# A third unit's local attention as matmuls, with other loads, another add of x and another mask

## The chip, the cores and the metric

The kernel runs on one core of a Trainium2 chip. The metric is the device time of one execution in microseconds; the median of three runs of the kernel before is 886.51 us (883.26 to 886.59).

## What is computed

The input is q, k, v of 4 batches, 8 heads, 576 positions, 64 dimensions. The attention is a sum of two parts, and two MLPs follow. Cut to what matters:

```python
def sm_attn(qq, kk, vv):                     # softmax attention
    ...
q_d, k_d, v_d = means over 4 neighbouring positions
out_up  = np.repeat(sm_attn(q_d, k_d, v_d), 4, axis=2)     # global: 144 positions
mask = np.abs(pos[:, None] - pos[None, :]) < 4             # local: 7 keys per query
out_local = softmax(np.where(mask, scale * q @ k.T, -1e9)) @ v
x = (out_up + out_local) as 2304 tokens x 512
h = np.maximum(np.maximum(x @ w1, x @ w2), x @ w3)         # 512 -> 768
y = h @ w_out                                              # 768 -> 512
g = y @ w_in;  out = np.maximum(0.01 * g, g) @ w_out2      # 512 -> 2048 -> 512
```

## The kernel before

The 2304 tokens are worked in 8 units of 288, two to a batch (unit u is a half of batch u // 2). Each unit passes through 22 steps: 18 steps of the first layer (6 blocks of 128 columns times three weight matrices, 12 matmuls of 128x288 each, since every product is made of three terms of a high and a low part), and 4 steps of the second layer, 18 matmuls each. Steps are counted through, g = 22 u + s. After unit 7 the second MLP runs in chunks of 512 tokens.

In L1_mm (L738) TensorE multiplies xh and xl, the high and low part of x, by the weights into ps_h; L1_post takes the largest of three products (ACT copies the first, VectorE's hm takes the maximum, L755) and splits it into hh (ACT) and hl (GpSimd, L759). L2 (L768) makes ps_o, which ACT copies out to memory (x2d).

The local attention, a window of seven keys, is made in two ways.

- Units 0 and 1 (u < PEU): on TensorE, a pair of heads at a time. pl_C puts a band mask and the scores into ps_ls, VectorE takes maxima and sums, ACT the exponential, GpSimd normalises, pl_O transposes (ps_lt), pl_P multiplies by v (ps_lo), pl_Q adds the global part on VectorE into x32, pl_R and pl_S split it into xh (ACT) and xl (GpSimd).
- Units 2 to 7: in the local stream, 12 items, two to a unit. GpSimd makes qkprod (L291, three to an item), VectorE (L301) and ACT (L304) sum it to scores ls, VectorE applies the mask to 21 of 63 columns (L310), a short softmax follows, VectorE makes pvprod (L335) and sums it to O (L342), three each. qkprod and pvprod share three buffers. emit_T then transposes O on TensorE (ps_x, L697, nine of them in three groups over two PSUM slots), VectorE adds the global part (L718) into the tile x32, ACT makes xh (L725), GpSimd xl (L726).

The global attention (names with ds) is made per batch and pair of heads: GpSimd or VectorE pools q and k (dsqk) and v (dsv), TensorE makes ps_sc, ps_aT and ps_up.

The order comes from three places. Up to the first layer of unit 0 a string, ORDER, lists the stages head by head, and all engines keep the order of the code. From then on only the queue of loads (SP) keeps it; the other engines are ordered by a scheduler before the run, and at run time each works through its own list in order. What is given to the scheduler at which step is set by tables: DONE and U1 spread the pieces of the local stream over the steps (the pools of the first way are released at step U1 = 15 and the stream's pools take their place), TURN says when emit_T of a unit comes, DS0 and DSOFF when the stages of the global attention come. The lines on which most rests:

```python
sl = s[:, 0:RC, :] if half == 0 else s[:, RU - RC : RU, :]
V.tensor_tensor(out=sl, in0=sl, in1=masks[half], op=ALU.min)
at(TURN[u], lambda u=u: emit_T(u))
```

## Time and profile before

| | |
|---|---|
| median of three runs | 886.51 us (883.26 to 886.59) |
| profiled execution, time | 885.25 us |
| its span | 883.4 us |
| mean granted clock of TensorE | 0.951 |
| TensorE busy | 825.4 us, 93% |
| VectorE busy | 490.2 us, 55% |
| ACT busy | 409.4 us, 46% |
| GpSimd busy | 292.0 us, 33% |

The time of an execution is a little more than the span of its instructions, here by 1.85 us. The shares are means over stages that differ much: in the page's 40 slices of 22 us TensorE is at 90% or more in most, and lower at the start and between the eighth and the thirteenth slice. What bounds a stage is read from that stage.

The names of the profile: PE is TensorE (its matmuls), PEld its weight loads, DVE VectorE, ACT ScalarE, POOL GpSimd, SP the engine that issues loads. A tile stands as out<-in by the program's names, L with a number is a line of the kernel.

### The profile page before, as it was taken

To read this page: it belongs to the slowest core of one execution; us is meant where nothing else is said; L and a number is where in the kernel's file an instruction comes from. 1 tells how busy PE (TensorE), PEld (TensorE's weight loads), DVE (VectorE), ACT (ScalarE), POOL (GpSimd) and SP (SyncE) were. 2 spreads that over 40 slices of the span, in tenths; PEclk is the share of its full clock that TensorE was granted. 3 is DMA by queue.
4 is the path that set the end of the run, shared out by engine and by line. 5 is a ranking of instruction groups with operands and counts; after the bars stand their busy time and mean duration, and the time that the engine had idled before them with its cause. 6 is when DMAs were issued, how large, how long until landed. Compare 5 with 4: busy or idle time off the path is not lost.

```text
span 883.4 us, 13548 instructions
## 1 busy us (share of the span) xinstructions
PE 825.4 (93%) x4886; PEld 726.5 (82%) x4890; DVE 490.2 (55%) x880; ACT 409.4 (46%) x1537; POOL 292.0 (33%) x263
## 2 busy tenths in 40 slices
...
GB/s 254 263 286 28 171 112 73 177 115 86 161 84 83 121 103 1 76 45 7 195 48 216 383 1 1 81 15 1 1 23 73 1 1 30 42 1 1 27 22 24
DMA packets 30486, 75.78 MB, mean 86 GB/s; under 512 B 3412, under 2 KB 8916, under 8 KB 30420
## 3 DMA queue, kind: packets, MB, share of 16 engines
...
q14 instruction: 29, 0.23, 0.1%
...
## 4 chain that ended last, share of the span: by engine, by line
PE 84%; DVE 6%; DMA 4%; ACT 3%; issue 1%; SPq 1%; ACTq 0%; DVEq 0%
PE ps_h L738 26%; PE acc L841 21%; PE ps_g L817 21%; PE ps_o L768 8%; DMA raw<-x2d 2%; PE ps_up L651 2%; DVE ls L310 2%; PE ps_sc L577 2%; ACT qkprod L304 2%; PE ps_lo L504 1%; PE ps_aT L629 1%; DMA skr<-in_kTp_dram 1%; PE ps_ls L429 1%; DVE x L718 1%; DVE pvprod L335 1%
## 5 line engine op out<-in xcount | busy, mean ns | idle before, releaser
L738 PE MATMUL ps_h<-xh,wA 128*128 128x288 f32 x1152 | 201.5, 306 | 17.9 <-ACT xh L725 10.9
L738 PEld LDWEIGHTS ps_h<-xh,wA 128*128 128x128 f32 x1152 | 172.4, 195 | 22.6 <-ACT xh L725 11.4
L841 PE MATMUL acc<-w2o,gh 128*128 128x512 f32 x576 | 178.1, 391 | 1.0 <-ACT gh L828 0.9
L817 PE MATMUL ps_g<-x2h,w2i 128*128 128x512 f32 (+1 forms) x640 | 158.9, 370 | 0.0
L825 DVE TENSOR_TENSOR g<-g,ps_g 128x512 f32<-128x512 f32 (+1 forms) x80 | 50.7, 634 | 185.1 <-ACT g L824 185.0
L817 PEld LDWEIGHTS ps_g<-x2h,w2i 128*128 128x128 f32 x640 | 114.6, 188 | 22.9
L824 ACT ACTIVATE g<-ps_g 128x512 f32<-128x512 f32 (+1 forms) x80 | 44.3, 553 | 186.2 <-PE ps_g L817 186.2
L841 PEld LDWEIGHTS acc<-w2o,gh 128*128 128x128 f32 x576 | 106.8, 188 | 23.8 <-ACT gh L828 1.9
L291 POOL TENSOR_TENSOR qkprod<-lq,lk 128x1344 f32<-128x1344 f32 x36 | 110.4, 3073 | 12.4 <-DVE O L342 4.4
L738 PE MATMUL ps_h<-xl,wA 128*128 128x288 f32 x576 | 113.6, 303 | 0.0
L841 PE MATMUL acc<-w2o,gl 128*128 128x512 f32 x288 | 112.2, 391 | 0.1
L738 PEld LDWEIGHTS ps_h<-xl,wA 128*128 128x128 f32 x576 | 90.9, 194 | 0.8 <-issue 0.8
L304 ACT ACTIVATE qkprod<-qkprod 128x64 f32<-128x64 f32 x364 | 87.6, 248 | 2.9 <-POOL qkprod L291 2.8
L755 DVE TENSOR_TENSOR hm<-hm,ps_h 128x288 f32<-128x288 f32 x96 | 43.0, 448 | 70.7 <-PE ps_h L738 65.3
L817 PE MATMUL ps_g<-x2l,w2i 128*128 128x512 f32 (+1 forms) x320 | 79.6, 370 | 0.0
L768 PE MATMUL ps_o<-hh,wO 128*128 128x288 f32 x384 | 75.3, 296 | 0.0
L829 DVE TENSOR_TENSOR gl<-g,gh 128x512 fp32r<-128x512 f32 (+1 forms) x80 | 51.0, 638 | 39.6 <-ACT gh L828 35.1
L759 POOL TENSOR_TENSOR hl<-hm,hh 128x288 fp32r<-128x288 f32 x48 | 40.5, 844 | 95.0 <-ACT hh L758 94.2
L304 ACT ACTIVATION_READ_ACCUMULATOR qkprod<-qkprod 128x1 f32 x364 | 70.6, 194 | 0.0
L828 ACT ACTIVATE gh<-g 128x512 fp32r<-128x512 f32 (+1 forms) x80 | 47.0, 588 | 42.7 <-DVE g L825 42.3
L817 PEld LDWEIGHTS ps_g<-x2l,w2i 128*128 128x128 f32 x320 | 56.8, 188 | 10.9
L841 PEld LDWEIGHTS acc<-w2o,gl 128*128 128x128 f32 x288 | 54.1, 188 | 12.6 <-DVE gl L829 0.9
...
## 6 DMA issues: line engine op xcount, KB each, us to landing
...
lv<-in_vL_dram SPq DMA_DIRECT2D x12, 480.0 KB, 4.6
lk<-in_k_dram SPq DMA_DIRECT2D x11, 480.0 KB, 4.5
...
```

The source lines that it names most:

```text
L291: P.tensor_tensor(out=pr, in0=in0, in1=in1, op=ALU.mult)
L304: A.activation(out=pr[:, r, j], in_=pr[:, r, j], func=AF.Copy, accum_out=sc[:, r, j : j + 1])
L738: T.matmul(out=ps, lhsT=wA[m, e][wi][:, kk * 128 : kk * 128 + 128], rhs=xx[:, kk] if u < PEU else xx[:, :, kk, :], start=n == 0, stop=n == ...
L755: V.tensor_tensor(out=t, in0=t, in1=ps, op=ALU.max)
L759: P.tensor_tensor(out=hl[:, m], in0=t, in1=hh[:, m].bitcast(F32), op=ALU.subtract)
L768: T.matmul(out=ps, lhsT=wO[m][wi][:, os_], rhs=xx[:, m], start=n == 0, stop=n == 3 * M1 - 1)
L817: T.matmul(out=ps, lhsT=w2i[m][wi][:, kk * 128 : kk * 128 + 128], rhs=xx[:, kk, :n], start=j == 0, stop=j == 3 * KC - 1,)
L824: A.activation(out=g, in_=ps, func=AF.Copy, scale=0.01)
L825: V.tensor_tensor(out=g, in0=g, in1=ps, op=ALU.max)
L828: A.activation(out=gh, in_=g, func=AF.Copy)
L829: V.tensor_tensor(out=gl, in0=g, in1=gh.bitcast(F32), op=ALU.subtract)
L841: T.matmul(out=accs[c, t], lhsT=a[:, ts], rhs=w, start=m == 0 and j == 0, stop=m == M2 - 1 and j == 2)
```

## The change

- PEU goes from 2 to 3: unit 2, the first half of batch 1, makes its local attention on TensorE, and batch 1's global attention is put into the same steps, 12 to 35 (table B1), that is beside units 0 and 1. The stages of unit 1 come one step later than before. dsqk of batch 1 is summed by VectorE (before, by GpSimd).
- The local stream has 10 items (6 to 15) and starts at step SUP = 37. Unit 3, the first of them, is laid out over contiguous positions ("whole"): its additions of the global part are 15 small ones.
- q and k of a pair of heads come in one load (tile sqk), v of both halves of a batch in one (sv, 344 KB in place of 168 KB ahead of the weights from the fourth on). The host lays out q, k, v of the local stream by lanes (qL, kL, vL), a load each.
- emit_T adds the global part to ps_x in place in PSUM; ACT makes xh from PSUM, and VectorE xl (before, GpSimd, from the tile x32). The slot of ps_x is in use until xl is done.
- The mask is 0 or a large negative number, added by GpSimd (before, the smaller of score and a large number, on VectorE).
- ON_A, the share of the score sums that ACT makes, holds for all items; in before the first four items had a smaller one. The string ORDER is arranged anew; in it the scores C of unit 1's first head come after twelve ps_h, where before they came ahead.

```diff
--- before.py
+++ after.py
-PEU = 2
+PEU = 3
-U1 = 15
+SUP = 37
...
-DONE = {2: 39, 3: 59, 4: 79, 5: 100, 6: 121, 7: 142}
-TURN = {2: 41, 3: 62, 4: 82, 5: 103, 6: 124, 7: 145}
-DS0 = {1: (15, 18, 21, 24), 2: (27, 38, 49, 60), 3: (68, 79, 90, 101)}
...
-ON_A_EARLY = (0, 7, 14)
+DONE = {3: 61, 4: 81, 5: 102, 6: 122, 7: 143}
+TURN = {3: 63, 4: 83, 5: 104, 6: 125, 7: 146}
+B1 = (12, 16, 20, 24)
+B1OFF = dict(A=0, v=1, C=1, B=2, L=4, O=6, M=7, P=9, N=10, Q=11)
+DS0 = {2: (39, 46, 53, 60), 3: (68, 79, 90, 101)}
 ON_A = (0, 21, 14)
...
-        P.memset(mk, 3.0e38)
+        P.memset(mk, 0.0)
...
-        V.tensor_tensor(out=sl, in0=sl, in1=masks[half], op=ALU.min)
+        P.tensor_tensor(out=sl, in0=sl, in1=masks[half], op=ALU.add)
...
+    def pl_load(what, b, h):
+        if what == "a":
+            t = sup.tile([128, 2 * S + 6], F32, tag="sqk", bufs=4, name="sqk")
+            nc.sync.dma_start(out=t, in_=qk[b, h])
+            dst[b, h, "q"], dst[b, h, "k"] = halves(t)
+            pl[b, h, "q"], pl[b, h, "k"] = t[:, :S], t[:, S:]
+        elif what == "s":
+            t = sup.tile([KP, 2, NBLK, 128], F32, tag="sv", bufs=4, name="sv")
+            n = PEU - 2 * b if b else 2
+            nc.sync.dma_start(
+                out=t[:, :n].rearrange("p u n d -> p (u n d)"), in_=vW[b, h][:, : n * NBLK * 128]
+            )
+            pl[b, h, "v"] = t
...
-            if b == 0:
+            if b < 2:
                 V.tensor_reduce(out=t[:, j], in_=raw, axis=AX.X, op=ALU.add)
...
-        groups = ((0, 4), (4, 8), (8, 9)) if half == 0 else ((0, 3), (3, 7), (7, 9))
+        whole = u == PEU
+        groups = ((0, 3), (3, 7), (7, 9)) if half and not whole else ((0, 4), (4, 8), (8, 9))
...
+                if whole:
+                    at_ = [(RU * c + r) // FAC for c in range(4)]
+                    for c0, nc_ in ((0, 4),) if len({at_[c + 1] - at_[c] for c in range(3)}) == 1 else ((0, 2), (2, 2)):
...
+                        V.tensor_tensor(out=sl, in0=sl, in1=in1, op=ALU.add)
...
-                sl = slice(r - g0, e - g0)
-                V.tensor_tensor(
-                    out=x32[:, sl].rearrange("p r (a c) -> p r a c", c=2),
-                    in0=pt[:, sl].rearrange("p r (a c) -> p r a c", c=2), in1=in1, op=ALU.add,
-                )
+                sl = pt[:, r - g0 : e - g0].rearrange("p r (a c) -> p r a c", c=2)
+                V.tensor_tensor(out=sl, in0=sl, in1=in1, op=ALU.add)
                 r = e
-            x32f = x32.rearrange("p r n -> p (r n)")
+            ptf = pt.rearrange("p r n -> p (r n)")
             xhf = xh[:, g0:g1].rearrange("p r a g -> p (r a g)")
-            A.activation(out=xhf, in_=x32f, func=AF.Copy)
-            P.tensor_tensor(
-                out=xl[:, g0:g1].rearrange("p r a g -> p (r a g)"), in0=x32f, in1=xhf.bitcast(F32), op=ALU.subtract
+            A.activation(out=xhf, in_=ptf, func=AF.Copy)
+            V.tensor_tensor(
+                out=xl[:, g0:g1].rearrange("p r a g -> p (r a g)"), in0=ptf, in1=xhf.bitcast(F32), op=ALU.subtract
             )
...
-        for what in "q0 k0 q1 k1 p0 q2 k2 00 p1 q3 k3 01 w0 p2 02 w1 p3 03".split():
+        for what in "a0 a1 p0 a2 s0 p1 a3 s1 w0 p2 w1 s2 p3 w2 s3".split():
...
         for h in range(4):
-            at(3 * h, lambda h=h: [f(1, h) for f in (pl_C, pl_D, pl_E, pl_H, pl_I)])
-            at(3 * h + 4, lambda h=h: [f(1, h) for f in (pl_O, pl_o)])
-            at(3 * h + 5, lambda h=h: [f(1, h) for f in (pl_P, pl_Q, pl_R, pl_S)])
+            at(3 * h + 1, lambda h=h: [f(1, h) for f in (pl_C, pl_D, pl_E, pl_H, pl_I)])
+            at(3 * h + 2, lambda h=h: pl_load("a", 1, h))
+            at(3 * h + 5, lambda h=h: [f(1, h) for f in (pl_O, pl_o)])
+            at(3 * h + 6, lambda h=h: [f(1, h) for f in (pl_P, pl_Q, pl_R, pl_S)])
+            at(3 * h + 7, lambda h=h: pl_load("s", 1, h))
+        for h in range(4):
+            for w, fs in {
+                "A": lambda h: ds_pool_qk(1, h),
+                "v": lambda h: ds_load(1, h, "v"),
+                "C": lambda h: [f(2, h) for f in (pl_C, pl_D, pl_E, pl_H, pl_I)],
+                "B": lambda h: [f(1, h) for f in (ds_B, ds_F, ds_G, ds_J, ds_norm)],
+                "L": lambda h: ds_pool_v(1, h),
+                "O": lambda h: [f(2, h) for f in (pl_O, pl_o)],
+                "M": lambda h: [f(1, h) for f in (ds_M, ds_m)],
+                "P": lambda h: pl_P(2, h),
+                "N": lambda h: [f(1, h) for f in (ds_N, ds_v)],
+                "Q": lambda h: [f(2, h) for f in (pl_Q, pl_R, pl_S)],
+            }.items():
+                at(B1[h] + B1OFF[w], lambda h=h, fs=fs: fs(h))
```

Three places show what this does to the order. The first is TensorE where the first unit of the local stream begins. In before that is unit 2; the end of unit 1's second layer (ps_o) and the first ps_h of unit 2:

```order
L768 MATMUL ps_o<-hl,wO_1351 128x288 x4
L577 MATMUL ps_sc<-dsqk 72x144 x2
L651 MATMUL ps_up<-aT,dsv_1735 128x144 x4
L629 MATMUL ps_aT<-ident,dse 72x72 x8
L651 MATMUL ps_up<-aT,dsv_1865 128x144 x4
L629 MATMUL ps_aT<-ident,dse 72x72 x8
L651 MATMUL ps_up<-aT,dsv_1974 128x144 x4
L577 MATMUL ps_sc<-dsqk 72x144 x4
L697 MATMUL ps_x<-ident,O 128x128 x9
L738 MATMUL ps_h<-xh,wA_0_439 128x288 x4
L738 MATMUL ps_h<-xh,wA_1_454 128x288 x4
L738 MATMUL ps_h<-xh,wA_2_605 128x288 x4
```

And now, where it is unit 3, between unit 2's ps_o and unit 3's ps_h:

```order
L741 MATMUL ps_o<-hl,wO_1391 128x288 x4
L616 MATMUL ps_up<-aT,dsv_2451 128x144 x4
L594 MATMUL ps_aT<-ident,dse 72x72 x8
L542 MATMUL ps_sc<-dsqk 72x144 x4
L663 MATMUL ps_x<-ident,O 128x128 x9
L616 MATMUL ps_up<-aT,dsv_2647 128x144 x4
L711 MATMUL ps_h<-xh,wA_0_398 128x288 x4
L711 MATMUL ps_h<-xh,wA_1_658 128x288 x4
```

The nine ps_x and the wait for them moved from unit 2 to unit 3, and most of the global attention that stood ahead of them is gone from there: between unit 1's last ps_o and unit 2's first ps_h the new order has nothing.

The second place is VectorE around the additions of the global part for unit 3 (u1 and u2 have none of these now). Before, line L718, with the mask behind them:

```order
L335 TENSOR_TENSOR pvprod<-lp,lv 128x1344
L613 RECIPROCAL dssum<-ps_sc 72x2
L342 TENSOR_REDUCE O<-pvprod 128x3x64
L718 TENSOR_TENSOR x_2859<-ps_x,up 128x128
L718 TENSOR_TENSOR x_2859<-ps_x,up 128x256
L310 TENSOR_TENSOR ls<-ls,mask_80 128x21
L314 TENSOR_REDUCE lp<-ls 128x9
L315 TENSOR_TENSOR lp<-ls,lp 128x63
L718 TENSOR_TENSOR x_2867<-ps_x,up 128x256 x2
```

Now, line L682, in PSUM, with the pvprod of item 9 ahead of them and no mask:

```order
L282 TENSOR_REDUCE lp<-lp 128x9
L283 TENSOR_SCALAR lp<-lp 128x9
L284 RECIPROCAL lsm<-lp 128x9
L285 TENSOR_TENSOR lp<-lp,lsm 128x63
L295 TENSOR_TENSOR pvprod<-lp,lv 128x1344
L682 TENSOR_TENSOR ps_x<-ps_x,up 128x128 x2
L302 TENSOR_REDUCE O<-pvprod 128x3x64
L682 TENSOR_TENSOR ps_x<-ps_x,up 128x32x2 x2
L295 TENSOR_TENSOR pvprod<-lp,lv 128x1344
L682 TENSOR_TENSOR ps_x<-ps_x,up 128x32x2 x2
```

The additions stand in the queue behind ten pvprods, three each of items 6, 7 and 8 and one of item 9, and between further ones.

The third is GpSimd at the start of the local stream: before, the first products (qkprod), with no mask among them:

```order
L566 TENSOR_TENSOR dsqk<-dsraw 128x144 x2
L759 TENSOR_TENSOR hl<-hm,hh 128x288
L291 TENSOR_TENSOR qkprod<-lq,lk 128x1344 x3
L565 TENSOR_TENSOR dsraw<-dsraw 128x144x2 x2
L291 TENSOR_TENSOR qkprod<-lq,lk 128x1344
L549 TENSOR_TENSOR dsrawv<-dsrawv 72x4x128
L565 TENSOR_TENSOR dsraw<-dsraw 128x144x2
```

Now, with the first mask, L270:

```order
L251 TENSOR_TENSOR qkprod<-lq,lk 128x1344 x3
L732 TENSOR_TENSOR hl<-hm,hh 128x288
L251 TENSOR_TENSOR qkprod<-lq,lk 128x1344
L530 TENSOR_TENSOR dsraw<-dsraw 128x144x2 x2
L514 TENSOR_TENSOR dsrawv<-dsrawv 72x4x128
L251 TENSOR_TENSOR qkprod<-lq,lk 128x1344
L531 TENSOR_TENSOR dsqk<-dsraw 128x144
L530 TENSOR_TENSOR dsraw<-dsraw 128x144x2 x2
L531 TENSOR_TENSOR dsqk<-dsraw 128x144
L270 TENSOR_TENSOR ls<-ls,mask_80 128x21
```

The mask of an item stands behind the next item's first two products and the pooling of batch 2.

## Rows read from the trace of the kernel before

**Rows 1.** Windows: us busy per engine (instructions), TensorE's granted clock, DMA share, GB/s
```profile
160.00:180.00 20.00, 12.08 (x52) 9.77 (x52) 15.73 (x30) 12.32 (x69) 18.01 (x11) 0.50 0.56 190
180.00:200.00 20.00, 8.33 (x36) 7.00 (x36) 19.04 (x21) 7.80 (x54) 15.13 (x16) 0.50 0.33 111
200.00:220.00 20.00, 20.00 (x125) 18.99 (x124) 17.33 (x31) 13.08 (x89) 17.29 (x13) 0.83 0.28 95
240.00:260.00 20.00, 16.13 (x108) 14.77 (x107) 16.42 (x24) 9.41 (x52) 14.91 (x14) 0.91 0.39 136
```

**Rows 2.** Timeline of TensorE, 150 to 200: start, duration, instruction, wait before it
```profile
154.90 1.15 PE L651 MATMUL ps_up<-aT,dsv 72*128 72x144 f32 x8
...
193.82 4.21 PE L738 MATMUL ps_h<-xh,wA 128*128 128x288 f32 x16 [10.91 <-ACT xh L725]
```

**Rows 3.** Chain that ended last, 300 to 480: start, duration, what
```profile
308.32 1.80 PE ps_h L738 x12
...
355.55 13.55 PE ps_h L738 x100
...
436.11 28.80 PE ps_h L738 x216
...
474.49 9.77 PE ps_g L817 x43
```

**Rows 4.** Timeline of TensorE, 55 to 72
```profile
55.67 0.41 PE L421 MATMUL ps_ls<-band,ident_b 96*96 96x306 bf16 x1 [6.45 <-DVE wy L190]
...
57.28 0.61 PE L738 MATMUL ps_h<-xh,wA 128*128 128x288 f32 x1
...
63.35 0.29 PE L421 MATMUL ps_ls<-band,ident_b 96*96 96x306 bf16 x1
...
64.27 0.40 PE L738 MATMUL ps_h<-xh,wA 128*128 128x288 f32 x1
...
66.99 0.66 PE L484 MATMUL ps_lt<-ident,ple 96*102 96x96 f32 x6
...
69.11 1.48 PE L504 MATMUL ps_lo<-plt,sv 102*128 102x96 f32 x12
70.37 0.38 PE L738 MATMUL ps_h<-xh,wA 128*128 128x288 f32 x1
```

**Rows 5.** The page's list of DMAs: count, size, us to landing
```profile
lk<-in_k_dram SPq DMA_DIRECT2D x11, 480.0 KB, 4.5
```

**Rows 6.** Groups by line and form, 100 to 480: count, busy us, mean ns, waits
```profile
L291 POOL TENSOR_TENSOR qkprod<-lq,lk 128x1344 f32<-128x1344 f32 x36 | 110.4, 3073 | 12.4 <-DVE O L342 4.4 <-DVE ls L301 3.6 <-ACT qkprod L304 3.4
...
L342 DVE TENSOR_REDUCE O<-pvprod 128x192 f32<-128x1344 f32 x36 | 55.3, 1544 | 0.2
...
L755 DVE TENSOR_TENSOR hm<-hm,ps_h 128x288 f32<-128x288 f32 x86 | 38.5, 448 | 68.0 <-PE ps_h L738 62.8 <-ACT wl L185 2.6 <-ACT hm L752 2.2
L759 POOL TENSOR_TENSOR hl<-hm,hh 128x288 fp32r<-128x288 f32 x43 | 36.5, 849 | 94.8 <-ACT hh L758 94.2 <-DVE hm L755 0.6
...
L310 DVE TENSOR_TENSOR ls<-ls,mask 128x21 f32<-128x21 f32 x12 | 23.1, 1924 | 0.9 <-ACT qkprod L304 0.9
...
L301 DVE TENSOR_REDUCE ls<-qkprod 128x21 f32<-128x1344 f32 x12 | 18.5, 1546 | 6.5 <-POOL qkprod L291 6.5
...
L591 DVE TENSOR_REDUCE ps_sc<-ps_sc 72x2 f32<-72x288 f32 x24 | 10.8, 457 | 13.0 <-PE ps_sc L577 12.9
...
L301 DVE TENSOR_REDUCE ls<-qkprod 128x7 f32<-128x448 f32 x12 | 7.3, 608 | 0.1
...
L315 DVE TENSOR_TENSOR lp<-ls,lp 128x63 f32<-128x63 f32 x12 | 2.7, 222 | 0.2
...
L718 DVE TENSOR_TENSOR x<-ps_x,up 128x128 f32<-128x128 f32 x6 | 2.3, 386 | 4.5 <-PE ps_x L697 4.5
```

**Rows 7.** Tile pvprod: count, shortest, median and longest ns, first and last start
```profile
L335 DVE TENSOR_TENSOR pvprod<-lp,lv x36: 1533/1548/1561, 125.2 to 352.6; 128x1344 f32<-128x1344 f32 x36
```

**Rows 8.** Tile ls: the same for the mask
```profile
L310 DVE TENSOR_TENSOR ls<-ls,mask x12: 167/1238/6574, 110.5 to 339.7; 128x21 f32<-128x21 f32 x12
```

More of the change, by code (lines that the diff above doesn't have):

```diff
@@ L135, in local_global_attention_moe_kernel @@
     sup = tc.alloc_tile_pool(name="sup", bufs=1, side="left")
-    pools = {0: sup}
+    pools = {0: sup, 1: sup}
     bands = []
-    for u in range(PEU):
+    for u in range(2):
         bd = sup.tile([QB, NBLK, KB], BF16, name=f"band{u}")
@@ L298, in qk_reduce @@
         sc = loc[i, "s"][:, c * RC : c * RC + RC, :]
-        nv = RC * WIN - (ON_A_EARLY if i < 2 * I0 else ON_A)[c]
+        nv = RC * WIN - ON_A[c]
         if nv:
@@ L401, in pl_load @@
             dst[0, h, "vr"] = t
-        pl[h, what] = t
     def pl_pool_v(h):
@@ L421, in pl_C @@
             T.matmul(
-                out=t[:QB, :n], lhsT=ident_b, rhs=bands[u].rearrange("p n k -> p (n k)"), start=True, stop=False
+                out=t[:QB, :n], lhsT=ident_b, rhs=bands[u % 2].rearrange("p n k -> p (n k)"), start=True, stop=False
             )
         for j in range(NBLK):
-            s0 = u * NCOL + j * QB
+            s0 = u % 2 * NCOL + j * QB
             qs, ks = slice(s0, s0 + QB), slice(s0, s0 + KB)
@@ L540, in ds_load @@
             nc.sync.dma_start(out=t.rearrange("p c h f d -> p (c h f d)"), in_=vP[b, h])
+            dst[b, h, w] = t
         else:
-            t = pools[b].tile([128, SD, FAC], F32, tag="mid", bufs=4, name="dsraw")
-            nc.sync.dma_start(out=t.rearrange("p s f -> p (s f)"), in_=(qT if w == "q" else kT)[b, h])
-        dst[b, h, w] = t
+            t = pools[b].tile([128, 2 * S + 6], F32, tag="dsraw", bufs=2, name="dsraw")
+            nc.sync.dma_start(out=t, in_=qk[b, h])
+            dst[b, h, "q"], dst[b, h, "k"] = halves(t)
     def ds_pool_v(b, h):
@@ L659, in ds_v @@
         if h == 0:
-            up[b] = pools[b].tile([128, 4, SD], F32, tag="up", bufs=2 if b else 1, name="up")
+            up[b] = mmp.tile([128, 4, SD], F32, tag="up", bufs=2, name="up")
         for hh in range(2):
@@ L669, in ds_stages @@
         return [
-            lambda: [ds_load(b, h, w) for w in "qk"],
+            lambda: ds_load(b, h, "qk"),
             lambda: ds_pool_qk(b, h),
@@ L856, in L4 @@
                     steps = [[G * DM, e - a], [DM, G]] if u < PEU else [[DM, e - a], [R * DM, G]]
+                    if u == PEU:
+                        row, steps = u * NCOL + r, [[DM, e - a], [RU * DM, G]]
                     nc.sync.dma_start(
@@ L870, in local_global_attention_moe_kernel @@
             else:
-                pl_load(what[0], int(what[1]))
-        for t in W1[2:nl]:
+                pl_load(what[0], 0, int(what[1]))
+        for t in W1[3:nl]:
             load_w1(t)
-        for h in range(4):
-            pl_load("1", h)
         steps = {
@@ L919, in local_global_attention_moe_kernel @@
         pieces = list(local_stream())
-        g0 = U1
+        g0 = SUP
         for u in range(PEU, NU):
```

123 lines of the change are left out of this document (43 added, 80 removed), and 8 rows, old and new, of the table ORDER.

## The prediction

> **What bounds the kernel now.** I read the windows first. Between 160 and 260 us TensorE is not full: it is busy 12.08, 8.33, 20.00 and 16.13 of 20 us in the four windows shown, at a granted clock of 0.50, 0.50, 0.83 and 0.91 [rows 1]. VectorE is full there instead, 15.73 to 19.04 of 20. Later windows have TensorE full at clock 1.00, and the second MLP, from 474.49 on, is a row of matmuls without gaps, which the change does not touch. So the stage to look at is the one in which local attention passes from TensorE to the VectorE stream.
>
> TensorE instruction by instruction shows it [rows 2]. Unit 1's second layer ends at 154.90; what follows is the global attention of batch 1, unit 2's transposes (ps_x), and a wait of 10.91 us before its first ps_h at 193.82. It is put down to ACT's xh, which waits for VectorE's adds. Until then TensorE did in 38.9 us what needs about 9. The chain gives lengths of undisturbed units [rows 3]: unit 7 takes 474.49 - 436.11 = 38.4, of which 28.80 is the first layer (1.6 a step, 18 steps) and 9.6 the second; unit 4, which carries a batch's global attention and a transpose, takes 355.55 - 308.32 = 47.2. A batch's global attention therefore costs at most 8.8, and the stretch from unit 4's start to unit 7's end 166.2.
>
> The forecast is worked along TensorE: when unit 1 ends, when unit 2 ends, when unit 3's x is there, and what follows.
>
> **Until unit 2 starts.** The local attention of unit 2 is new work on TensorE. One head beside L1 costs: C (ps_ls) 64.27 - 63.35 = 0.92, twice; O (ps_lt) at most 0.66; P 70.37 - 69.11 = 1.26 [rows 4]. That is 3.8 a head, 15.0 for four. Batch 1's global attention, which stood behind 154.90, moves ahead of unit 1's end: 8.8. In the prologue the first ps_h stood behind C, which started at 55.67 after a wait of 6.45; now twelve ps_h stand ahead of it. That can give back at most 57.28 - 55.67 = 1.6 [rows 4]. Against it, 688 KB more of v are loaded ahead of the weights from the fourth on; I take a gain of 1.0, with 1.6 and -3 as ends. Unit 2 starts at 154.9 + 15.0 + 8.8 - 1.0 = 177.7. The one-load q and k and the host's lanes save issues on SP, which is waited for nowhere in this stretch: nothing.
>
> **Unit 2.** 38.4, plus about half of batch 2's global attention, 4.4 (its heads start at steps 39 to 60): it ends at 220.5. No ps_x stands before it, so the 38.9 us between [rows 2]'s two instructions go, but for the 8.8 counted above, and the half clock that followed goes too.
>
> **When unit 3's x is there.** The local stream starts at step 37, not 15, since its pools reuse those of the TensorE path. Its k load waits for the last xl of unit 2, step 35; four steps and a second layer, 4 x 1.6 + 9.6 = 16.0, lie between that and unit 2's start, and a k load lands 4.5 after its issue [rows 5]. First product on GpSimd: 177.7 - 16.0 + 4.5 = 166.2.
>
> From there it is a queue on GpSimd and then one on VectorE. Item 6's mask, now on GpSimd, stands behind five products of 3.07 and eight smaller steps; at hl's 0.85 for each [rows 6] it comes 22 us in, and with 2 us of softmax the first pvprod starts 24 us in. Unit 3's x adds stand on VectorE behind the tenth pvprod (items 6 to 8 and one of item 9). Between the first and the tenth the order has 9 pvprods of 1.55 [rows 7] and 9 O reduces of 1.54, 27.8; 3 score reduces of 1.55 and 3 of 0.61, 6.5; 18 softmax steps of 0.22, 4.0; 7 hm of 0.45, 3.1; 4 reduces of 0.46 and 16 tiny steps at 0.17, the shortest mask, 4.5: together 45.9 [rows 6 to 8]. VectorE was busy 68.5 of 80 us in [rows 1], and 95% in the window in which TensorE waited most; at 92% the 45.9 take 50. The adds come in 15 pieces with two pvprods, three O reduces, two score reduces and the three xl among them: 3.1 + 4.6 + 2.2, adds at 0.3 (0.39 for 128 columns, twelve are half as wide) 4.5, xl at most 1.8 by hm's 0.45 for 288 columns: 16.2, and 0.5 for xh. Unit 3 can start at 166.2 + 24 + 50 + 16.7 = 256.9, and TensorE waits 36 us, once, with only the tail of batch 2's attention to do.
>
> That xl goes from GpSimd to VectorE and now holds the PSUM slot until it is done is in these 16.2: the third transposes wait for the first xl. With two units in flight later it is covered by matmuls; uncovered it would cost one xl, 0.8 a unit.
>
> **After that.** The wait leaves the clock at half: after 193.82 the clock was 0.50 to 200 and 0.83 in the next window, 6.2 x 0.5 + 20 x 0.17 = 6.5 lost [rows 1]. Unit 3 takes 38.4 + 6.5 + 2.8 (a transpose and some global attention) = 47.7, units 4 to 7 the 166.2 of before. End of the first MLP: 470.8, 3.7 before the 474.49 of now. The small waits of unit 3 in before need no term, since 47.7 has none: most came behind long masks on VectorE, which go. From the profiled 885.25 this gives 881.5; it lies 1.3 under the median of the runs, and I say 881.
>
> **The mask.** VectorE's mask takes 1.92 us in the mean for 21 columns, 0.167 to 6.574 [rows 6, 8]: it is not work but waiting, and GpSimd was busy 15 to 18 of 20 us [rows 1]. On GpSimd I price it at 0.2, the shortest on VectorE; bounds are 0.17 and, if GpSimd waits in its place, 1.92. Its other price is order, the 22 us above.
>
> The Trainium skill (SBUF — State Buffer, section "Who interferes with whom") says that a VectorE tensor_tensor with both inputs in SBUF and a GpSimd instruction that reads SBUF exclude each other for a whole instruction, and that issue order decides who waits. The mask rows agree; pvprod, of the same kind, does not: all 36 lie between 1533 and 1561 ns [rows 7] beside a GpSimd as busy. By the rule pvprod and qkprod would keep taking turns, the mask's move would gain nothing, and the time would be the first rival's; by the rows it gains the 1.7 us an item.
>
> **Rivals.** *The stream keeps its pace.* In before a pvprod came every (352.6 - 125.2) / 35 = 6.5 us [rows 7]. Then the ten take 65 instead of 50, unit 3 starts at 272, and the end is at 485.8: 897. The break-even is 5.4 a pvprod. For it: products and pvprods still share three buffers, so each engine waits for the other, and GpSimd has the masks besides. Against it: 0.64 of the 6.5 was the mask, and part of the 36 were paced by TensorE's steps later on, where lateness cost nothing. The late start has no reserve: whatever the stream loses, TensorE loses one for one. Chance 0.25.
>
> *The stream runs at VectorE's rate.* First pvprod at 21, ten at 4.6, the adds in 12.5: unit 3 starts at 246 and the end is at 460, so 871. For it: TensorE asks for no hm while it waits, and there are no mask stalls. Against it: in-order queues on three engines, with an exp on ACT in each softmax. Chance 0.20.
>
> *Units 0 and 1 swell.* Two units with four heads took 97.6 in before, 76.8 + 15.0 and 5.8 of friction. With twice the heads, batch 1's attention and its pooling on VectorE, friction doubles: everything behind moves by 5.8, to 887. For it: each head is a chain through four engines, and a late one stops TensorE, which is in order. Against it: VectorE and GpSimd have no local stream there now. Chance 0.21. The forecast has 0.34.
>
> **How the numbers follow.** A measurement of this kernel tells 0.5%, 4.4 us, from no change. The forecast is 5 us under the median, its own range 874 to 888; of its 0.34 I count 0.24 as faster and 0.10 as no change. The second rival adds 0.20 faster. The third gives 0.19 no change and 0.02 slower, the first 0.23 slower and 0.02 no change. Sums: 0.44, 0.31 and 0.25. The range reaches from the second rival's 871, less the clock's 6.5 that a shorter wait would save in part, to just over the first's: 865 to 898.
>
> **What the profile after would show.** Right: no ps_x between unit 1 and unit 2, ps_h running on; one long idle on TensorE before unit 3's first ps_h, 30 to 40 us, released by ACT's xh, with the half clock around it and nowhere else before the second MLP; masks of 0.2 us on GpSimd; pvprods about 5 us apart until then. Wrong: a wait under 20 us with the first pvprods 4.6 apart (second rival), one of 45 or more with GpSimd and VectorE waiting for each other's products (first), or gaps of one or two us between the ps_h of steps 12 to 40 (third). An idle ahead of units 5 to 7 would say that the stream is too slow throughout, which I count out.

## The result: slower by 1.3%, and the profile after

The changed kernel took 898.05 us (median of 4, 895.51 to 899.23) beside 886.55 of the kernel before: ratio 1.0134, interval 1.0101 to 1.0167. The forecast of 881 was wrong in its sign; 898.05 lies 0.05 above the end of the stated range, beside the 897 of the first rival. The profiled execution took 899.23, 13.98 more than that of before.

The windows of the changed kernel, with the columns of [rows 1]:

```profile
180.00:200.00 20.00, 18.16 (x125) 17.32 (x124) 7.60 (x18) 11.98 (x81) 14.49 (x16) 0.91 0.18 63
200.00:220.00 20.00, 20.00 (x155) 19.82 (x155) 17.93 (x28) 12.62 (x88) 16.39 (x15) 1.00 0.33 111
220.00:240.00 20.00, 9.59 (x59) 7.56 (x57) 16.52 (x26) 12.48 (x87) 15.82 (x13) 0.72 0.52 174
240.00:260.00 20.00, 2.39 (x9) 1.75 (x9) 18.52 (x38) 14.09 (x105) 19.31 (x13) 0.50 0.21 76
...
300.00:320.00 20.00, 15.20 (x102) 14.16 (x102) 14.61 (x22) 13.11 (x86) 17.56 (x14) 0.86 0.41 141
320.00:340.00 20.00, 20.00 (x143) 19.30 (x143) 18.69 (x33) 13.01 (x88) 15.62 (x10) 0.97 0.33 106
```

The wait that stood at 160 to 200 in [rows 1] now stands at 225 to 263, as forecast. Below full again is 300 to 320, with TensorE busy 15.20 at clock 0.86; from 320 to 340 it is busy throughout at 0.97. In before both windows have 20.00 at 1.00. Instruction by instruction on TensorE, with the columns of [rows 2]:

```profile
179.56 0.80 PE L711 MATMUL ps_h<-xh,wA 128*128 128x288 f32 x4 [1.33 <-ACT ev L744]
...
186.71 0.81 PE L711 MATMUL ps_h<-xh,wA 128*128 128x288 f32 x4 [1.83 <-ACT ev L744]
...
224.38 0.69 PE L741 MATMUL ps_o<-hl,wO 128*128 128x288 f32 x4
...
245.03 1.94 PE L663 MATMUL ps_x<-ident,O 128*128 128x128 f32 x8 [5.08 <-DVE dssum L578]
258.91 0.45 PE L663 MATMUL ps_x<-ident,O 128*128 128x128 f32 x1 [11.94 <-DVE xl L699]
...
262.85 3.50 PE L711 MATMUL ps_h<-xh,wA 128*128 128x288 f32 x13
...
313.47 1.64 PE L711 MATMUL ps_h<-xh,wA 128*128 128x288 f32 x8 [3.46 <-ACT xh L698]
```

Unit 2 starts at 179.56 with no ps_x before it and a gap of 1.33; its last ps_o is issued at 224.38; unit 3's transposes come at 245.03, the last at 258.91, after 11.94 us for the slot that VectorE's xl holds; unit 3 starts at 262.85. Then unit 4 waits too, 3.46 for its xh, and 1.20 for ev. The starts of the units (first ps_h, from the timelines; the forecast's from its sum), us:

| | unit 2 | unit 3 | unit 4 | unit 5 | unit 6 |
|---|---|---|---|---|---|
| before | 193.8 | 250.7 | 308.3 | 355.5 | 396.5 |
| forecast | 177.7 | 256.9 | 304.6 | 351.8 | 392.9 |
| after | 179.6 | 262.9 | 313.5 | 365.0 | 410.7 |

From unit 6 on both kernels take the same. So 14.3 were gained by unit 2's start; the lead turned into 12.2 lost at unit 3's start, 5.2 lost at unit 4's, 9.5 at unit 5's and 14.1 at unit 6's.

### The profile page after: what moved, and what is told of

Same layout as the page of the kernel before. It is cut to its first block, busy times and chain, and to the rows that moved or that the text cites. A ratio compares the mean times of both kernels' runs of the same rounds, so it can differ in the third digit from the quotient of the medians.

```text
span 897.4 us, 13812 instructions
## 1 busy us (share of the span) xinstructions
PE 831.7 (93%) x5005; PEld 731.2 (81%) x5009; DVE 465.7 (52%) x912; ACT 414.7 (46%) x1556; POOL 258.6 (29%) x240
## 4 chain that ended last, share of the span: by engine, by line
PE 76%; DMA 8%; DVE 7%; ACT 3%; issue 2%; POOL 2%; SPq 1%; ACTq 0%; DVEq 0%; POOLq 0%
PE acc L814 21%; PE ps_g L790 21%; PE ps_h L711 20%; PE ps_o L741 6%; DMA lk<-in_kL_dram 2%; DMA x2d<-ev 2%; ACT qkprod L264 2%; PE ps_lo L468 1%; PE ps_up L616 1%; PE ps_sc L542 1%; POOL qkprod L251 1%; DMA raw<-x2d 1%; DMA wO<-in_w_out_dram 1%; PE warm_ps L166 1%; DVE pvprod L295 1%
## 5 line engine op out<-in xcount | busy, mean ns | idle before, releaser
L251 POOL TENSOR_TENSOR qkprod<-lq,lk 128x1344 f32<-128x1344 f32 x30 | 91.8, 3070 | 14.0 <-DMA lk<-in_kL_dram 4.8
L264 ACT ACTIVATE qkprod<-qkprod 128x64 f32<-128x64 f32 x350 | 84.1, 246 | 21.4 <-POOL qkprod L251 21.0
L741 PE MATMUL ps_o<-hh,wO 128*128 128x288 f32 x384 | 77.2, 297 | 0.0
L264 ACT ACTIVATION_READ_ACCUMULATOR qkprod<-qkprod 128x1 f32 x350 | 67.2, 192 | 0.0
```

The source lines that it names most:

```text
L251: P.tensor_tensor(out=pr, in0=in0, in1=in1, op=ALU.mult)
L264: A.activation(out=pr[:, r, j], in_=pr[:, r, j], func=AF.Copy, accum_out=sc[:, r, j : j + 1])
L741: T.matmul(out=ps, lhsT=wO[m][wi][:, os_], rhs=xx[:, m], start=n == 0, stop=n == 3 * M1 - 1)
```

## The experiments

Each kernel is the changed one with the edit that is named, unless it says "the kernel before". Ratios are to the kernel before, with the interval; the last columns are the starts of units from one profile. Every edit is scheduled anew, so the order of the engines moves with it. Counted in the traces, the additions of units 3, 4 and 5 begin behind 10, 19 and 27 pvprods in the changed kernel, 7, 19 and 26 in e1, 9, 19 and 26 in e3, 10, 18 and 25 in e4, 9, 18 and 26 in e5, 8, 16 and 24 in e15, 10, 17 and 25 in e16. No run holds the order fixed: a gain belongs to an edit together with the order that came with it.

| run | ratio | unit 3 | unit 4 | unit 5 | unit 6 |
|---|---|---|---|---|---|
| the change | 1.0134 (1.0101 to 1.0167) | 262.9 | 313.5 | 365.0 | 410.7 |
| e1 emit_T 61 | 1.0044 (1.0019 to 1.0069) | 244.7 | 307.8 | 355.9 | 400.8 |
| e2 emit_T 58 | 1.0118 (1.0058 to 1.0178) | 247.2 | 312.2 | 362.3 | 408.8 |
| e3 mask VectorE | 1.0047 (1.0007 to 1.0088) | 257.6 | 310.7 | 355.6 | 399.8 |
| e4 x SBUF, xl GpSimd | 0.9961 (0.9931 to 0.9990) | 257.0 | 307.6 | 353.4 | 396.9 |
| e5 e3 and e4 | 0.9974 (0.9937 to 1.0011) | 251.0 | 309.6 | 355.6 | 400.3 |
| e6 e5 and e1 | 1.0032 (0.9999 to 1.0064) | 240.9 | 314.3 | 361.5 | 404.3 |
| e7 x SBUF, xl VectorE | 1.0066 (1.0027 to 1.0105) | 255.9 | 307.0 | 358.9 | 401.7 |
| e8 two dsrawv | 1.0057 (1.0032 to 1.0083) | 260.4 | 311.8 | 359.4 | 404.9 |
| e9 four products | 1.0152 (1.0105 to 1.0199) | 257.0 | 310.1 | 368.6 | 414.8 |
| e10 e9 and e3 | 1.0041 (1.0006 to 1.0077) | 245.6 | 301.8 | 350.8 | 400.5 |
| e11 two pvprods | 0.9837 (0.9776 to 0.9898) | 244.3 | 294.2 | 340.1 | 385.7 |
| e12 two qkprods | 0.9968 (0.9939 to 0.9997) | 252.4 | 302.0 | 349.0 | 395.7 |
| e13 before, mask GpSimd | 0.9799 (0.9764 to 0.9834) | 236.7 | 283.9 | 333.9 | 376.7 |
| e14 before, x PSUM | 1.0078 (1.0050 to 1.0106) | 253.9 | 306.6 | 355.9 | 401.5 |
| e15 e4, 21 on ACT | 1.0005 (0.9983 to 1.0027) | 243.2 | 301.3 | 351.9 | 397.1 |
| e16 e4, 7 on ACT | 0.9929 (0.9902 to 0.9955) | 252.5 | 301.7 | 347.4 | 390.1 |
| e17 before, both edits | 0.9864 (0.9823 to 0.9905) | 241.2 | 291.4 | 339.4 | 386.1 |
| e18 e13, 7 on ACT | 0.9705 (0.9678 to 0.9731) | 236.9 | 283.5 | 329.6 | 373.2 |

**The order of unit 3's additions.** e1, and e2 with its stream pieces earlier too:

```diff
-TURN = {3: 63, 4: 83, ...
+TURN = {3: 61, 4: 83, ...
```

> The changed kernel with emit_T of unit 3 given to the scheduler two steps earlier (TURN 61 in place of 63). In the order unit 3's additions then stand on VectorE behind 7 pvprods in place of 10. Theory (order): the late start of unit 3 comes from the queue, in which work for unit 4 stands ahead of unit 3's additions. At the 5.3 us a pvprod that the changed kernel shows there, the additions come 3 x 5.3 = 16 us earlier, unit 3's first ps_h at about 247 in place of 262.9, and the time falls by 12 to 16, to 882 to 886. Rival (pace): the stream as a whole is too slow; unit 3 starts earlier, but units 4 and 5 wait for it by as much more, and the time stays at 894 to 898.

```diff
-DONE = {3: 61, ...
-TURN = {3: 63, ...
+DONE = {3: 57, ...
+TURN = {3: 58, ...
```

> The changed kernel with the pieces for unit 3 given to the scheduler by step 57 (DONE 57) and its emit_T at 58. The additions stand behind 6 pvprods, which is all of items 6 and 7 and nothing else, and the transposes ahead of unit 2's last four ps_o. Theory (order): another pvprod less, 5 us, so unit 3 starts 18 to 21 earlier than in the changed kernel, at 242 to 245, and the time is 877 to 882. Rival (pace): 892 to 898, with TensorE waiting before units 4 and 5. A third way: transposes that are not ready hold back ps_o on TensorE, and it is slower than with emit_T at 61.

Unit 3 started 18.1 earlier in e1, as the order theory has it, but unit 4 only 5.7 earlier. TensorE in e1, the same columns:

```profile
243.46 0.45 PE L663 MATMUL ps_x<-ident,O 128*128 128x128 f32 x1 [9.95 <-DVE lsm L284]
...
304.62 0.44 PE L663 MATMUL ps_x<-ident,O 128*128 128x128 f32 x1 [3.56 <-DVE xl L699]
...
307.77 1.57 PE L711 MATMUL ps_h<-xh,wA 128*128 128x288 f32 x5 [1.29 <-ACT xh L698]
```

The 11.94 before the last of unit 3's transposes became 9.95. Of the 18.1 us 12.4 were given back between unit 3's start and unit 4's: by the timelines 5.6 is a busy TensorE, with a head of the global attention that in the changed kernel stood ahead of unit 3, and 6.8 are waits, 4.7 of them ahead of a ps_up and 2.1 for xl and xh of unit 4 (5.6 in place of 3.5). So the order explains unit 3's start, and the pace only a part of what became of it; e1 kept 8 us of 18. In e2 the third way came true in part: it is slower than e1, and transposes wait for the slot for 18.7 us, in two pieces (waits of TensorE, 220 to 330):

```profile
PE ps_x L663 <- DVE xl L699: 18.7, 2, 13.3
```

**The two side edits undone.**

```diff
-        P.tensor_tensor(out=sl, in0=sl, in1=masks[half], op=ALU.add)
+        V.tensor_tensor(out=sl, in0=sl, in1=masks[half], op=ALU.min)
```

> The changed kernel with the mask as before: the smaller of score and large number, on VectorE. Theory (the mask's place in GpSimd's queue): the first pvprod came 30 us after the first product, of which 6 are the mask's wait behind products; they go, and unit 3 starts up to 6 earlier, 892 to 896. Rival (the shared access to SBUF): the mask on VectorE waits 1.9 us in the mean again, ten times, four of them before unit 3's additions, and it is slower by 4 to 8, 901 to 906.

```diff
+            x32 = mmp.tile([128, 512], F32, tag="x32t", bufs=2, ...)
-            V.tensor_tensor(out=sl, in0=sl, in1=in1, op=ALU.add)
+            V.tensor_tensor(out=so, in0=sl, in1=in1, op=ALU.add)     # so: in x32
-            V.tensor_tensor(out=xl..., in0=ptf, in1=xhf, op=ALU.subtract)
+            P.tensor_tensor(out=xl..., in0=x32, in1=xhf, op=ALU.subtract)
```

> The changed kernel with x as before: the sum goes to an SBUF tile, and GpSimd makes xl. Theory: the place of xl matters little, since three xl of 0.7 us stand in VectorE's queue; between 894 and 900. Rival: in the changed kernel the third group of unit 3's transposes waited 11.9 us for the first xl, which holds the PSUM slot; with an SBUF tile the slot is free after the additions, so unit 3 starts some us earlier and each later unit too: 888 to 893.

e3's mask waits on VectorE as before, up to 5.3 us (tile ls, columns of [rows 7]), and yet the kernel is 10 us faster than the changed one; its first pvprod starts at 190.8, 7 us earlier than in the changed kernel:

```profile
L270 DVE TENSOR_TENSOR ls<-ls,mask x10: 173/868/5319, 184.4 to 349.0; 128x21 f32<-128x21 f32 x10
```
```profile
L295 DVE TENSOR_TENSOR pvprod<-lp,lv x30: 1533/1551/1558, 190.8 to 361.1; 128x1344 f32<-128x1344 f32 x30
```

e4 gained more than its rival allowed, 15 us: the 11.94 before unit 3's last transpose became 1.73, and TensorE has no idle time left in units 4 and 5 (unit starts as windows, columns of [rows 1]):

```profile
307.57:353.44 45.87, 45.87 (x346) 44.42 (x346) 40.98 (x72) 35.44 (x227) 34.09 (x26) 1.00 0.23 72
353.44:396.91 43.47, 43.47 (x330) 42.74 (x329) 18.18 (x32) 11.30 (x33) 8.91 (x10) 1.00 0.19 64
```

Together they do not add, as e5 and e6 show:

> The changed kernel with both the mask on VectorE (e3) and x by an SBUF tile with xl on GpSimd (e4). Theory: two separate waits, the mask behind GpSimd's products and the PSUM slot held by ps_x; their effects (10 and 15 us) add in good part: 872 to 878. Rival: both only shorten the same wait, the late x of units 3 to 5, and together give hardly more than e4 alone: 880 to 884.

> e5 with emit_T of unit 3 two steps earlier as in e1: unit 3's additions stand behind 7 pvprods in place of 9. Theory (order): since units 4 and 5 now get their x in time, the 10 us that unit 3 starts earlier are kept at the end: 862 to 870. Rival (pace): as in e1 unit 4's start takes most of it back: within 3 us of e5.

e5 is no better than e4, as its rival says. A reason stands in its masks: with xl on GpSimd again, the ten masks on VectorE take 28.7 us (in e3 17.9), the longest 9.05 (columns of [rows 6]):

```profile
L270 DVE TENSOR_TENSOR ls<-ls,mask 128x21 f32<-128x21 f32 x10 | 28.7, 2867 | 0.8 <-ACT qkprod L264 0.8
```

In e6 unit 3 starts at 240.9, 22 earlier than in the changed kernel, and unit 4 at 314.3, later; it is 5 us slower than e5, which neither answer foretold, and it does not show the pace. Its masks take 37.6 us. One of them stands among unit 4's additions on VectorE; ACT's aT waits in order behind the softmax that follows it, and TensorE for aT:

```profile
301.21 6.90 DVE L270 TENSOR_TENSOR ls<-ls,mask 128x21 f32<-128x21 f32 x1
```
```profile
308.85 2.29 PE L616 MATMUL ps_up<-aT,dsv 72*128 72x144 f32 x8 [6.72 <-ACT aT L606]
```

The earlier emit_T with x in SBUF and the mask on GpSimd was not run. e7 parts what e4 joined (edit of e4, with xl left on V):

> The changed kernel with the sum written to an SBUF tile as before, but xl still on VectorE. It tells apart the two things that e4 undid. Theory (slot): what cost time is that ps_x keeps its PSUM slot until xl is done, so the next transposes and the global attention's ps_aT and ps_up wait; the gain of e4 stays with xl on VectorE: 882 to 887. Rival (engine): three xl of 0.7 us more per unit in VectorE's queue are what cost; 894 to 899.

At 892.59 (interval of the ratio 1.0027 to 1.0105) it lies between the two answers: by the ratios some 0.7% is the slot and 1.0% the engine of xl, each to about half a per cent.

**The queue of loads.**

```diff
-            t = pools[b].tile([QP, 2, 2, FAC, D], F32, tag="dsrawv", bufs=1, name="dsrawv")
+            t = pools[b].tile([QP, 2, 2, FAC, D], F32, tag="dsrawv", bufs=2, name="dsrawv")
```

> The changed kernel with two buffers in place of one for the tile dsrawv. In the changed kernel the queue of loads stood still for 83.7 us, up to 25.1 at a time, because a load of dsrawv waited until GpSimd had made dsv, and the next k loads of the stream stood behind it. Theory (load queue): with a second buffer those loads go out earlier, GpSimd no longer waits for lk, and units 4 and 5 get their x earlier: 890 to 894. Rival: loads are early enough, since GpSimd waited for lk for only 4.8 us in all: 896 to 899.

891.86, as the theory says of the time. GpSimd still waits 3.2 us for lk, in place of 4.8, and units 4 and 5 start 1.7 and 5.6 earlier. The wait of the loads (engine, line, releaser, us, times, longest), changed kernel and then e8:

```profile
SPq L504 <- POOL dsv L515: 83.7, 5, 25.1
```
```profile
SPq L504 <- POOL dsv L515: 30.8, 3, 14.3
```

It is not quite clean: in e8's order unit 3's additions stand behind 9 pvprods, not 10.

**What paces the stream.**

```diff
-        pr = pools["att"].tile([128, RC, WIN, D], F32, tag="prod", bufs=3, name="qkprod")
+        pr = pools["att"].tile([128, RC, WIN, D], F32, tag="prod", bufs=4, name="qkprod")
```

> The changed kernel with four buffers in place of three for the products (qkprod and pvprod share them). In all kernels so far unit 4 starts between 307 and 314 us, however early unit 3 starts (241 to 263), and an item of the stream takes 20.5 us in the changed kernel as in the one before. Theory (coupling): no engine is full, GpSimd and VectorE wait for each other's product buffers; a fourth one quickens the stream to 18 us an item or less, unit 4 starts before 306, and the time is 888 to 892. Rival (work): the stream is set by the sum of the instructions in VectorE's queue, and the buffer changes nothing: 896 to 899.

> e9 with the mask on VectorE as in e3. If the mask's place on GpSimd and the product buffers are two waits, their gains add to e3: 878 to 883. If both are the same waiting of VectorE for GpSimd's queue: as e3, 886 to 890.

(20.5 there is first product to last pvprod, divided by the items.) Coupling by the buffers falls: e9 is no faster than the changed kernel (901.53, above even the rival's range), and e10 is as e3. In e10 units 3 and 4 do start 12 and 9 us before those of e3, but unit 6 at 400.5 does not. The two probes take work away instead:

```diff
     def pv_mult(i, c):
+        if c == RU // RC - 1:
+            return
...
     def qk_mult(i, c):
+        if c == 1:
+            loc[i, "pr", 1] = loc[i, "pr0"]
+            return
```

> A probe: the changed kernel without the third pvprod and O sum of each item (ACT copies the first third of O in their place), 3.1 us an item less on VectorE, 31 in all. If VectorE's work sets the stream's pace, an item takes about 17 in place of 20.5 us, unit 4 starts 10 to 13 earlier (near 301), and the time falls by 12 to 16, to 882 to 886. If GpSimd sets it: under 4 us.

> A probe: the changed kernel without the second qkprod of each item (the score sums take the first product in its place), 3.1 us an item less on GpSimd, 31 in all, with every other engine's work as it is. If GpSimd's queue sets the stream's pace, an item takes about 17 us, unit 4 starts near 301 and the time is 882 to 886. If VectorE sets it: under 4 us, 895 to 899. If both e11 and e12 gain half of that, the two engines pace each other.

e11 gained 25 us, more than the 12 to 16 expected, e12 14 us, as expected if GpSimd sets the pace. So work taken from either engine shortens the time, from VectorE more; no one engine sets it alone. e11's pvprods, 20 in place of 30, end 26 us earlier than the changed kernel's:

```profile
L297 DVE TENSOR_TENSOR pvprod<-lp,lv x20: 1543/1554/1558, 198.7 to 346.2; 128x1344 f32<-128x1344 f32 x20
```

**The side edits by themselves,** in the kernel before (the edits of e3 and e4 the other way round):

> The kernel before with the mask as a sum on GpSimd and nothing else. Theory (queue): on GpSimd a mask stands behind products, and the softmax on VectorE behind it, in this kernel too; it costs 3 to 10 us: ratio to before 1.004 to 1.012. Rival (shared access): VectorE's 23 us of waiting in masks go, and units 2 to 4 get their x earlier: ratio 0.985 to 0.996.

> The kernel before with x added in PSUM and xl made by VectorE from it, and nothing else. Theory (slot and VectorE's queue): the slot of ps_x is held until xl is done and VectorE has 1.5 us more a unit; it costs here too, ratio 1.004 to 1.015. Rival: it costs only where x is late as in the changed kernel: ratio 0.998 to 1.002.

> The kernel before with both side edits, the mask on GpSimd and x added and split in PSUM, and units 0 and 1 alone on TensorE. If the edits add: 0.980 x 1.008 = 0.988 of before. If they hinder each other, as in the changed kernel, where the two together are slower than either alone: 0.995 or more. In the first case the changed kernel's loss against this one, 1.0134 / 0.988 = 1.026, is the third unit on TensorE with its late stream; in the second it is in good part the two edits.

The mask's move alone makes the kernel before 2.0% faster, against my theory. (In the two profiles 1.6 us of it stand already at unit 1's first ps_h, 110.94 against 112.58, ahead of the stream's first mask.) Its mask there (tile ls) and TensorE ahead of unit 2:

```profile
L310 POOL TENSOR_TENSOR ls<-ls,mask x12: 221/231/262, 116.0 to 322.7; 128x21 f32<-128x21 f32 x12
```
```profile
176.25 1.09 PE L697 MATMUL ps_x<-ident,O 128*128 128x128 f32 x4 [6.51 <-DVE ps_sc L612]
...
183.63 4.21 PE L738 MATMUL ps_h<-xh,wA 128*128 128x288 f32 x16 [4.30 <-ACT xh L725]
```

Of the 10.91 in [rows 2] 4.30 are left; the longest mask of before, 6.57 [rows 8], had stood in that wait. x in PSUM costs 0.8% there, and both together come to 0.9864, against 0.980 x 1.008 = 0.988: they add. Set side by side:

| | two units on TensorE | three units |
|---|---|---|
| mask VectorE, x in SBUF | 1 (before) | 0.9974 (e5) |
| mask GpSimd, x in SBUF | 0.9799 (e13) | 0.9961 (e4) |
| mask VectorE, x in PSUM | 1.0078 (e14) | 1.0047 (e3) |
| both | 0.9864 (e17) | 1.0134 (after) |

The third unit, with the loads and the order that belong to it, changes nothing while the mask is on VectorE (0.9974, and 1.0047 / 1.0078 = 0.997), and costs 1.7 to 2.7% with the mask on GpSimd (0.9961 / 0.9799 = 1.017, 1.0134 / 0.9864 = 1.027).

**Less work for VectorE, nothing left out.**

```diff
-ON_A = (0, 21, 14)
+ON_A = (0, 21, 21)     # e15;  e16 and e18: (7, 21, 14)
```

> e4 (the changed kernel with x in SBUF and xl on GpSimd) with all 21 scores of an item's third part summed on ScalarE: 0.61 us an item less on VectorE, 1.7 more on ScalarE. e11 gave 25 us for 3.1 us an item. Theory (VectorE's work sets the stream): 0.61 x 8 = 5 us less than e4, ratio to before 0.988 to 0.993. Rival: ScalarE, busy two thirds there, becomes what the softmax waits for: ratio 0.996 to 1.004.

> e4 with 7 of 21 scores of an item's first part summed on ScalarE as well: 0.47 us an item less on VectorE, 1.7 more on ScalarE. Theory (VectorE's work): 4 us less than e4, ratio to before 0.989 to 0.995. Rival (ScalarE): ratio 0.996 to 1.004.

> The kernel before with the mask on GpSimd and, from item 8 on, 7 of 21 scores of an item's first part summed on ScalarE (as in e16), 0.47 us an item less on VectorE. If VectorE's work still sets the time of units 3 to 5: 2 to 4 us less than e13, 0.975 to 0.978 of before. If after the mask's move TensorE is full from unit 3 on, nothing is left to gain: 0.979 to 0.981.

e16's ratio lies 0.32% under e4's, about 3 us, with intervals that overlap: the sign is that of VectorE's share, the gain is not clear of noise. e18's lies 0.94% under e13's, clear of it, but 8 us by the ratios and 5 by the medians are more than the 2 to 4 us foretold, so VectorE's 0.47 us an item are not all of it. e15 gains nothing, as the rival says. The scores that it moves are an item's last, which the softmax waits for; that this is the cause was not shown. e18, 861.71 us, is the fastest version, 3.0% below the kernel before.

## Why the prediction was wrong

**Until unit 2 starts**: 179.56 against 177.7, but by two misses of opposite sign, so that the closeness is luck in part. The thirteenth ps_h, the one behind the first twelve, started at 54.28, in before at 60.1 (the second of the two in the second row):

```profile
54.28 0.61 PE L711 MATMUL ps_h<-xh,wA 128*128 128x288 f32 x1
```
```profile
60.02 0.42 PE L738 MATMUL ps_h<-xh,wA 128*128 128x288 f32 x2
```

That is 5.9 earlier, where the forecast took 1.0 and allowed 1.6: C itself came at 52.66 in place of 55.67, with the twelve done ahead of it. From there to unit 2's first ps_h TensorE took 125.3, against 94.8 to the 154.90 of before: 30.5 more, not 15.0 + 8.8 = 23.8. By the timelines the added matmuls of the local and the global attention took 22.6, near their price; TensorE waited 5.8 us there in place of 2.4.

**Unit 2**: 45.5 us against 42.8. Three loads of the stream (lq, lk and dsraw of 288, 480 and 579 KB) were issued between 176.65 and 177.51, just ahead of the output of unit 1. The chain shows ACT's ev behind ACT's score sums, and then a write of 6.33 where the median of before is 1.8:

```profile
178.07 1.14 ACT qkprod L264 x9
179.22 0.59 ACT ev L744 x2
...
179.90 6.33 DMA x2d<-ev
```

The first is the 1.33 in the timeline above; the next ev waits for the write, and ps_h for it: the 1.83. The clock of 0.91 in the window from 180 to 200 follows it. In the end this cost nothing, since TensorE then waited for unit 3's x.

**When unit 3's x is there**: 262.9 against 256.9. The first product came at 167.4 (forecast 166.2), the ten pvprods took 48.1 (50) and additions and split 17.0 (16.7). The first pvprod was 30.3 after the first product, not 24. VectorE in that stretch (columns of [rows 2]):

```profile
170.56 1.55 DVE L261 TENSOR_REDUCE ls<-qkprod 128x21 f32<-128x1344 f32 x1 [2.62 <-POOL qkprod L251]
...
188.28 0.23 DVE L274 TENSOR_REDUCE lp<-ls 128x9 f32<-128x63 f32 x1 [2.91 <-POOL ls L270]
...
193.23 0.23 DVE L282 TENSOR_REDUCE lp<-lp 128x9 f32<-128x63 f32 x1 [4.47 <-ACT lp L276]
...
197.79 3.01 DVE L295 TENSOR_TENSOR pvprod<-lp,lv 128x1344 f32<-128x1344 f32 x2
```

It waits for the mask behind GpSimd's queue, as the forecast had it, and then 4.47 for an exp that stands on ACT behind the next item's 21 sums, which the forecast had not. e3, with the mask on VectorE, has 21.7 there; but e4, with the mask on GpSimd, has 28.0 and e5, with it on VectorE, 26.5, so the mask's place is not all of it.

**After that**: here the sum failed. It gave unit 3 47.7 and units 4 to 7 "the 166.2 of before". They took 50.6 and 488.6 - 313.5 = 175.2 (488.6 is the end of the last ps_o). Of the 17.9 by which the end of the first MLP was missed (488.6 against 470.8), 11.9 are this step, 6.0 the x of unit 3. From start to start, with the columns of [rows 1], units 3, 4 and 5 of the changed kernel, and units 4 and 5 of before:

```profile
262.85:313.47 50.62, 47.15 (x348) 45.62 (x347) 39.51 (x69) 34.65 (x232) 39.15 (x32) 0.96 0.36 121
313.47:364.97 51.50, 49.30 (x349) 46.87 (x349) 38.87 (x74) 32.10 (x203) 30.56 (x23) 0.93 0.25 81
364.97:410.68 45.71, 44.65 (x334) 43.40 (x334) 23.70 (x38) 11.16 (x34) 5.94 (x7) 1.00 0.17 54
```
```profile
308.25:355.48 47.23, 47.23 (x353) 45.07 (x352) 42.17 (x68) 30.13 (x186) 28.93 (x23) 1.00 0.17 52
355.48:396.54 41.06, 41.06 (x314) 41.04 (x314) 12.26 (x27) 11.03 (x32) 8.88 (x10) 1.00 0.21 64
```

TensorE was idle for 3.5, 2.2 and 1.1 us in units 3 to 5, in units 4 and 5 of before not at all. The rest is a busy TensorE: the clock fell to 0.93 behind the wait for unit 4's x, and unit 5 has 334 matmuls in place of 314, global attention that came later than in before. An "idle ahead of units 5 to 7", the forecast's own sign of a stream that is too slow throughout, hardly came: 0.4 us ahead of unit 5, none ahead of 6 and 7.

The term behind it is the price of x in PSUM with xl on VectorE, if uncovered "one xl, 0.8 a unit". With that edit undone (e4) units 4 and 5 have no idle time, unit 3 starts at 257.0 (forecast 256.9), units 4, 5 and 6 at 307.6, 353.4 and 396.9 (304.6, 351.8 and 392.9), and the time is 882.79: 15 of the 17 us between 881 and 898.05, order included. That e4 comes out near the forecast does not confirm the rest of it: the mask's move gives 2.0% by itself (e13), and beside that the third unit costs 1.7%.

The forecast's lengths had a second weakness. In before the stream had begun 63 us earlier than in the changed kernel (104.3 and 167.4) with only two more items to make, so before's units 4 to 7 say nothing on a stream that starts late. The pace was near that of before: the pvprods, columns of [rows 7],

```profile
L295 DVE TENSOR_TENSOR pvprod<-lp,lv x30: 1533/1547/1558, 197.8 to 372.1; 128x1344 f32<-128x1344 f32 x30
```

came every (372.1 - 197.8) / 29 = 6.0 us, against 6.5 in [rows 7]; 5.3 up to unit 3's start, 6.3 behind it. With that unit 4 starts at 307 to 314 in the changed kernel and in e1 to e9 alike, with unit 3 started anywhere from 241 to 263: what quickens unit 3 is given back at unit 4, in e1 mostly to global attention, in e6 to a mask. Less work in the stream moves unit 4 to 294 to 302 (e11, e12, e16). e10 and e15 have it at 301.8 and 301.3 too, but unit 6 no earlier than e3 and e4, so unit 4's start alone does not tell the end.

The first rival's 897 was right by luck. It put the loss ahead of unit 3, at 272 (262.9), and counted ten intervals from the first pvprod to the tenth where the forecast's 45.9 counts nine. Nine of 6.5 make 58.5: unit 3 at 265.4 and the end at 890. Its break-even is then (50 + 3.7) / 9 = 6.0 an interval, passed only behind unit 3. And its reason, the shared buffers, fell (e9).

One link of the late pace is in the chain of the changed kernel:

```profile
260.97 2.27 PE ps_up L616 x8
...
263.31 0.74 POOL dsv L515
264.07 0.33 SPq L504
...
265.86 8.70 DMA lk<-in_kL_dram
...
277.72 3.08 POOL qkprod L251
...
282.70 3.05 POOL qkprod L251
...
286.31 1.55 DVE pvprod L295
...
288.01 1.15 POOL dse L583
289.16 0.70 POOL dsv L515
289.88 0.33 SPq L504
...
291.67 6.94 DMA lk<-in_kL_dram
...
310.86 5.75 DMA x2d<-ev
```

The first time a ps_up on TensorE, in order behind the transposes that wait for xl, frees dsv; only then does GpSimd make the next dsv, only then does the load of dsrawv go out, and behind it in the load queue the k of an item that is due: 8.70 and 6.94 us until it lands. e8 shortens this link (83.7 to 30.8 us of standing still) and gains 6 us, e4 shortens it too (56.3). The last row is the write that unit 4's 1.20 for ev waits for.

**The mask**: the row was read rightly and the place wrongly. On GpSimd it takes 0.22 us:

```profile
L270 POOL TENSOR_TENSOR ls<-ls,mask x10: 213/222/259, 188.0 to 351.3; 128x21 f32<-128x21 f32 x10
```

That is worth 2.0% in the kernel before, where the waits in [rows 8] stood on the path. In the changed kernel the same move gained nothing (e4 against e5) or lost (after against e3). That a late stream has no slack for a mask in GpSimd's queue fits the 30.3 against 21.7 us; but see e4 and e5 above. The interplay with x in PSUM is 1.0% (1.0134 x 0.9974 / (0.9961 x 1.0047) = 1.010), in the kernel before none. The masks go with it: taking xl off GpSimd shortens the masks on VectorE from 28.7 us (e5) to 17.9 (e3) in the changed kernel, and only from 23.1 to 20.5 (e14) in the kernel before. That this is all of it was not tested.

**The rule weighed against the rows**: the rows held. pvprod stayed at 1533 to 1558 ns beside GpSimd's work, and the mask alone on GpSimd gained time (e13). By the Trainium skill's rule (SBUF — State Buffer, "Who interferes with whom") the prediction had reckoned, on the rival's side, that it would gain nothing. That the pace stayed slow has the causes above.

**The other points.** The third rival, units 0 and 1 swelling by 5.8, came true in size: 6.7 more than the forecast's 23.8, hidden by the earlier start. But only 3.4 are added waits, and the sign that it named, gaps between the ps_h of steps 12 to 40, did not show: the waits for heads, 1.32 and 0.98 for plt, lie ahead of these steps. "Uncovered it would cost one xl, 0.8 a unit" was far too small: before a unit that waits anyway it was part of 11.94 us, since the xl stands in VectorE's order behind pvprods. x in PSUM costs 0.8% in the kernel before. And the last step from 881.5 to 881 went the wrong way: a profiled run 1.3 under the median makes it 882.8 against the median.
